# A new written order for a fused gated-attention and MLP kernel: the same steps at other places in the engines' queues

## The chip, the cores and the metric

The kernel runs on one core of one Trainium2 chip. Its engines take their instructions from separate queues, each strictly in order, and wait for one another by semaphores: PE multiplies matrices, DVE and POOL work elementwise, ACT applies functions and copies, SP issues transfers. The metric is the device time of one execution in microseconds (us). Times are given as the median of several executions. Beside them stands one execution under the profiler, and all durations of single instructions come from it.

## The reference

Two stages, in float32. A gated linear attention carries a 48 x 48 state for each of 4 x 8 (batch, head) pairs through 768 tokens; its output, put back as 3072 tokens of 384 numbers, goes through an MLP whose activation is `h * cos(h)`.

```python
B, H, S, D = 4, 8, 768, 48
for t in range(S):
    state = alpha[:, :, t, :, None] * state + einsum('bhd,bhe->bhde', k[:, :, t], v[:, :, t])
    y[:, :, t] = einsum('bhd,bhde->bhe', q[:, :, t], state)
x = y.transpose(0, 2, 1, 3).reshape(3072, 384)
h = x @ w_in            # 384 x 2048
out = (h * cos(h)) @ w_out      # 2048 x 384
```

## The kernel before

The 3072 tokens are cut into 12 jobs J0 to J11 of 256 tokens (three for each batch). A job holds two chunks of 128 rows; in J0 and J1, which are loaded together in another layout, a digit in a step's name after the kind can also mean a quarter or a half of the heads. Every piece of work is a named step, a small function that issues one or some instructions:

- `load a/k/q/v` (SP, lines 124 and 134) brings in the inputs of a job, 384 KB each; `w1` and `w2` (POOL's transfer queue, lines 150 and 156) bring in four parts of each weight, u0 to u3.
- `ln` (ACT, line 174) takes the logarithm of alpha; `mula` (POOL, line 180) first multiplies neighbouring gates. `cq`, `cd`, `cums0`, `cums` (PE) sum the logarithms with triangular matrices, `sub` (DVE, line 239) forms a difference. `icp` and `exps` (ACT, lines 250 and 256) take exponentials; `eb` stands for a job's four exponentials and the next job's `ln`.
- `sk` and `sq` (lines 269 and 273) multiply k and q by these exponentials: 128 x 384 float32, both operands in SBUF. `:D` after a date puts a step on DVE, `:A` on ACT; without a letter `sk` and `sq` run on POOL. `castv` (line 283) converts v.
- `trans` (PE, lines 342 and 352) transposes the scaled q and k, `evT` (lines 359 and 362) evicts the result, `scores` (PE, line 370) multiplies them, `mask` (DVE, line 375) masks the scores. `vpe` and `vev` (lines 301 to 316), or `vst` by transfers (SP, line 289), stack v.
- `outer` (PE), `decay` (POOL, line 325), `add` (DVE, line 411) and `state` (line 420) carry the state from chunk to chunk. `yT` (PE, line 446) makes the attention's output, `evy` (line 456) evicts it.
- `m1 u` (PE, line 465, 12 matmuls of 256 columns), `sin u` (ACT, line 471, on 128 x 1024), `gate u` (DVE, line 476) are the first half of the MLP; `m2` (PE, lines 487 and 493, 4 matmuls of 384 columns each) is the second, `evo` (lines 500 and 502) evicts it and `out` (SP, line 510) stores it. `idle` (PE, line 518) multiplies zeros.

What decides the order is the table `PLAN`: for each step one date per job, `-` where a job has no such step. The program sorts all steps by date and issues them so; a date is only a key for sorting, and nothing waits for a date. Each engine then runs its instructions in that order, and the tile framework adds the semaphores.

```python
    with tc.manual_schedule():
        for _, _, kind, args in sorted(order, key=lambda x: x[:2]):
            steps[kind](*args)
```

Two pools of PSUM matter for waiting. Tag `h` has three slots of two banks, shared by T_ps, A_ps, U_ps, y_ps and the MLP's h_ps, so that an `m1` can only begin when the step that reads an older slot is done. Tag `o` has one slot: the next `m2` chain begins when `evo` has emptied it. A wait is kept per tile: a writer of one half of a two-bank tile waits for earlier readers of the other half.

Of the kernel before, what the change touches and what calls it, by code (L numbers as in the profile page):

```python
# [16 lines left out]
def kernel(  # L17
# [11 lines left out]
    B, H, S, D = q.shape  # L29
# [78 lines left out]
    w1 = consts.tile([C, KT, DF], BF, tag="w1", name="w1")  # L108
    w2 = consts.tile([C, NF, DM], BF, tag="w2", name="w2")
# [404 lines left out]
    def idle(n):  # L514
# [18 lines left out]


    PLAN = {
# [73 lines left out]
    }  # L609
    IDLE = [(1201, 11), (5915, 1), (9015, 20), (13611, 2), (18367, 3)]  # L610

    order = []
    for key, line in PLAN.items():
        kind, *rest = key.split()
        for J, word in enumerate(line.split()):
            if word != "-":
                t, _, eng = word.partition(":")
                args = [J] + [int(x) if x.isdigit() else x for x in rest] + [{"A": "ACT", "D": "DVE", "P": "POOL"}[x] for x in eng]
                order.append((int(t), len(order), kind, args))
    for t, n in IDLE:  # L620
        order.append((t, len(order), "idle", [n]))
# [34 lines left out]
```

## Time and profile before

| what | value |
|---|---|
| median of 3 executions | 193.19 us (190.25, 193.44, 193.19) |
| the profiled execution, its own time | 190.47 us |
| its span, first to last instruction | 188.8 us |
| granted PE clock, mean | 0.996 |
| PE busy | 178.0 us, 94% of the span |
| DVE busy | 136.1 us, 72% |
| ACT busy | 128.8 us, 68% |
| POOL busy | 75.3 us, 40% |
| moved by transfers | 29.48 MB, mean 156 GB/s |

The span is what the profile divides into instructions; the execution's own time is 1.7 us longer. Busy shares are averages over the whole span. An engine with 72% can be full in one stretch and idle in another, so the profile is read by stretches of time, and after that by what an engine waited for.

### The profile page before, as it was taken

Reading aid. Unit: us, or ns where it says so; the run is one execution under the profiler, and the core shown is the slowest. Engines: PE = TensorE matmul, PEld = TensorE weight load, DVE = VectorE, ACT = ScalarE, POOL = GpSimd, SP = SyncE. Lnnn points to the kernel's source line nnn. Section 1 sums busy time; section 2 is a strip of 40 time slices with the busy share of each in tenths; the row PEclk is TensorE's granted clock in tenths of the full one; section 3 lists DMA queues with packets and bytes.
Section 4 is the critical chain, followed back from the end, with each engine's and each line's share of the span. In section 5 each row is a group of like instructions: output and inputs, shape, how many; then the busy total and the mean of one; then the engine's idle time right before and its main releaser. Section 6 shows DMA issues by size and latency. Waiting matters only on the chain.

```text
span 188.8 us, 5950 instructions
## 1 busy us (share of the span) xinstructions
PE 178.0 (94%) x2543; PEld 129.7 (69%) x2546; DVE 136.1 (72%) x183; ACT 128.8 (68%) x166; POOL 75.3 (40%) x111
## 2 busy tenths in 40 slices
PE   7898989989999999999999999999999999999990
PEld 2555776846578686786688668576686686777770
DVE  7086887657998989488978987978558686562640
ACT  4374685799689989889778999547844573373530
POOL 7085900167749163584494089070620501000000
PEclk9999999999999999999999999999999999999998
DMA  5979999999978849959998874034050000450313
GB/s 173 320 207 144 198 174 153 265 283 244 318 193 230 230 122 244 256 139 288 233 286 235 225 181 121 9 69 115 23 120 2 5 0 3 107 119 11 77 41 83
DMA packets 56570, 29.48 MB, mean 156 GB/s; under 512 B 43360, under 2 KB 56544, under 8 KB 56544
## 3 DMA queue, kind: packets, MB, share of 16 engines
q1 hardware_dynamic: 52672, 25.86, 51.8%
q0 software_dynamic: 3712, 3.15, 11.2%
q8 instruction: 20, 0.33, 0.7%
q10 hardware_dynamic: 160, 0.10, 0.2%
q14 instruction: 6, 0.05, 0.1%
HBM read 25.17 MB, written 4.72 MB: 158 GB/s over the span
## 4 chain that ended last, share of the span: by engine, by line
PE 72%; ACT 10%; DVE 8%; DMA 4%; issue 2%; SPq 1%; DVEq 0%; ACTq 0%
PE h_ps L465 31%; PE o_ps L493 26%; PE y_ps L446 5%; DMA q<-in_q_dram 4%; PE A_ps L370 2%; DVE kh L269 2%; ACT c_sb L471 2%; DVE gsb L476 2%; PE T_ps L352 2%; PE U_ps L398 2%; DVE xT L456 2%; PE o_last L487 1%; ACT cp L256 1%; ACT L165 1%; ACT L471 1%
## 5 line engine op out<-in xcount | busy, mean ns | idle before, releaser
L476 DVE TENSOR_TENSOR gsb<-h_ps,c_sb 128x1024 bf16<-128x1024 f32 x48 | 58.3, 1222 | 20.2 <-ACT c_sb L471 18.6
L471 ACT ACTIVATE c_sb<-h_ps,halfpi 128x1024 bf16<-128x1024 f32 x48 | 53.1, 1113 | 21.8 <-PE h_ps L465 21.2
L493 PE MATMUL o_ps<-w,gsb 128*128 128x384 bf16 x368 | 66.7, 326 | 0.9 <-DVE o_sb L502 0.6
L465 PE MATMUL h_ps<-xT,w 128*128 128x256 bf16 x576 | 66.2, 272 | 1.2 <-ACT xT L456 0.7
L465 PEld LDWEIGHTS <-w 128*128 128x128 bf16 x576 | 55.7, 98 | 9.8 <-issue 1.7
L493 PEld LDWEIGHTS <-gsb 128*128 128x128 bf16 x368 | 33.9, 98 | 22.0 <-issue 1.3
L375 DVE TENSOR_TENSOR A_sb<-A_ps,msk 128x1024 bf16<-128x1024 f32 x24 | 28.8, 1214 | 1.9 <-PE A_ps L370 1.9
L420 POOL TENSOR_TENSOR un<-us,c 128x384 bf16<-128x384 f32 x16 | 14.0, 873 | 35.5 <-DVE us L411 35.5
L273 POOL TENSOR_TENSOR qh<-q,cp 128x384 bf16<-128x384 f32 x15 | 14.9, 999 | 13.1 <-DMA q<-in_q_dram 13.1
L273 POOL TENSOR_TENSOR kh<-k,icp 128x384 bf16<-128x384 f32 x15 | 15.2, 1021 | 4.3 <-ACT icp L250 4.3
L180 POOL TENSOR_TENSOR a<-a 128x384 f32<-128x384 f32 x9 | 9.3, 1031 | 15.3 <-DMA a<-in_alpha_dram 15.3
L502 ACT COPY o_sb<-o_ps 128x384 f32<-128x384 f32 x12 | 5.8, 480 | 12.6 <-PE o_ps L493 9.6
L362 ACT COPY qkT<-T_ps 128x1024 bf16<-128x1024 bf16 x10 | 9.7, 1017 | 3.6 <-DVE qkT L362 2.1
L518 PE MATMUL idle_ps<-zeros 128*128 128x512 bf16 x34 | 10.5, 461 | 1.7 <-DVE zeros L53 1.3
L456 DVE CAST xT<-y_ps 128x384 bf16<-128x384 f32 x13 | 7.0, 553 | 6.4 <-ACT xT L456 4.5
L174 ACT ACTIVATE lna<-a 128x768 bf16<-128x768 f32 x12 | 10.1, 846 | 2.1 <-DMA a<-in_alpha_dram 2.1
L165 ACT ACT_TABLE_LOAD x8 | 10.3, 1283 | 0.9 <-PEq L640 0.8
L471 ACT ACT_TABLE_LOAD x8 | 10.3, 1283 | 0.1
L411 DVE TENSOR_TENSOR us<-U_ps,un 128x384 f32<-128x384 f32 x16 | 8.8, 552 | 1.8 <-PE U_ps L398 1.8
L502 DVE COPY o_sb<-o_ps 128x384 f32<-128x384 f32 x11 | 6.1, 553 | 5.5 <-PE o_ps L493 5.5
L370 PE MATMUL A_ps<-qkT 48*128 48x128 bf16 x192 | 9.0, 218 | 1.1 <-DVE gsb L476 0.4
L370 PEld LDWEIGHTS <-qkT 48*128 48x128 bf16 x192 | 5.8, 94 | 4.8 <-issue 2.6
(91 smaller groups left out, 179.1 us busy)
## 6 DMA issues: line engine op xcount, KB each, us to landing
a<-in_alpha_dram SPq DMA_DIRECT2D x12, 384.0 KB, 4.7
q<-in_q_dram SPq DMA_DIRECT2D x12, 384.0 KB, 5.2
k<-in_k_dram SPq DMA_DIRECT2D x12, 384.0 KB, 5.5
v<-in_v_dram SPq DMA_DIRECT2D x12, 384.0 KB, 4.5
out_dram<-o_sb SPq DMA_DIRECT2D x38, 96.0 KB, 2.2
vs<-vp SPq DMA_DIRECT2D x36, 64.0 KB, 2.6
w<-in_moe_w_in_dram POOLq DMA_DIRECT2D x4, 384.0 KB, 6.3
w<-in_moe_w_out_dram POOLq DMA_DIRECT2D x4, 384.0 KB, 8.0
```

The lines of the kernel that those rows point to most:

```text
L165: nc.scalar.preload_act_table_set("natural_log_exp_and_others")
L273: eng.tensor_tensor(out=x[J % NQ][:, e, :, 0:D], in0=kqv[nm, J][:, :, e], in1=f, op=ALU.mult)
L370: nc.tensor.matmul(A_ps[J, c][:, a, p, :], qkT[r, c, NP + p, :], qkT[r, c, p, :], start=True, stop=True)
L375: nc.vector.tensor_tensor(out=A_sb[J][:, c].rearrange("s a p t -> s (a p) t"), in0=A_ps.pop((J, c)).rearrange("s a p t -> s (a p) t"), in1 ...
L420: eng.tensor_tensor(out=u, in0=new, in1=c2_sb[J][:, :, c].unsqueeze(3).to_broadcast([C, NP, 2, D]), op=ALU.mult)
L456: copy(out=xT[J][:, :, c * C : (c + 1) * C], in_=y_ps[J][:, c, 0 : KT * C].rearrange("r (i t) -> r i t", i=KT))
L465: nc.tensor.matmul(h_ps[J, u][:, f, :], w1[:, kk, ft * C : (ft + 1) * C], xT[J][:, kk, :], start=(kk == 0), stop=(kk == KT - 1))
L471: nc.scalar.activation(out=c_sb[J, u], in_=h_ps[J, u], func=AF.Sin, bias=halfpi, scale=1.0)
L476: nc.vector.tensor_tensor(out=gsb[J][:, u * FW : (u + 1) * FW], in0=h_ps.pop((J, u)), in1=c_sb.pop((J, u)), op=ALU.mult)
L493: nc.tensor.matmul(o_ps[J, c][:, 0:DM], gsb[J][:, ft, c * C : (c + 1) * C], w2[:, ft], start=(ft == 0), stop=(ft == NF - 1))
L502: copy(out=o_sb[J, c], in_=o_ps.pop((J, c))[:, 0:DM])
L518: nc.tensor.matmul(idle_ps[0], zeros[:, 0:C], zeros, start=True, stop=True)
```

## The change

Only the dates in `PLAN`, the letters behind them and the list `IDLE` are others; every function stays, and every step of before is there once. PE has one more matmul of zeros (38 for 37). On PE the order differs up to about date 48,000, the beginning of `yT J2`; behind it PE's steps stand in the same order to the end. On the other engines steps change their places throughout, and forty change the engine: ten of `sk` and `sq` go from POOL to DVE and four from DVE to POOL, `castv J2` goes from POOL to ACT, thirteen evictions go from DVE to ACT and twelve from ACT to DVE. SP issues loads in another order relative to the stores, and POOL issues the parts of the weights as u2, u3, u0, u1 and u0, u3, u2, u1 (before: u2, u0, u1, u3 and u0, u1, u2, u3). The core of the diff:

```diff
     PLAN = {
...
-        "load a": "750 1320 27620 28190 29330 37741 44441 56807 66187 68447 74447 82487",
-        "w1": "10835 12726 9645 13576",
-        "w2": "17133 18763 19613 20463",
-        "sub": "- - - 39720 45836 51846 61530 76810 84617 92106 106190 119199",
-        "icp 0": "6915 9600 37604 - - - - - - - - -",
-        "exps 0": "7290 8725 38854 - - - - - - - - -",
-        "sk 0": "9210:D 11254:D 38651:D 41651 48351 66435:D 71598 82909 94573 107068 109918 129216",
-        "sk 1": "10718:D 11968:D 39049 42535:D 53753 63201 77427 81983:D 90096 108018 108968 131692:D",
-        "sq 0": "8545 8545:D 40192 43621:D 49851 65101 72548 87426 89566:D 110996:D 118996 128266",
-        "sq 1": "11685 9926:D 40195:D 43151:D 52803 62251 76307 88376 91123 103448 117876 130336",
-        "castv": "11710:A 13291:A 35881 46851 55551 57441 78377 92853 89326 106298 119946 141140",
-        "vev": "- - 41200 - - - - - - - - -",
-        "vev 1": "16476:A 21611 - - - - - - - - - -",
-        "decay": "10665 10495 40022 42601 56321 77257 79147 82739 104398 118826 130166 127316",
-        "evT 0": "13831 18156:A 42569:A 45891:A 59319 70018:A 83329:A 91501 110391 115839 129342 140188:A",
-        "yT": "19166 26750 48173 56676 71150 89916 89286 107371 123000 135506 148672 161541",
-        "evy 0": "20016 27740 49163:D 57764:D 72140 90906 90486 108361:D 123990 138375:D 149785 162531:D",
-        "evy 1": "19996:D 27740:D 49163 58844:D 72140:D 90906:D 90116 108836:D 123990:D 137900:D 150155 162531",
-        "m1 2": "24684 32304 52639 59692 77257 95330 102636 118310 131457 147259 156839 163732",
-        "m2 0 0": "26002 39990 55275 69096 82407 99284 113085 124915 136231 149557 160793 172269",
-        "m2 0 1": "27635 40643 55928 69749 83060 99937 113738 125568 136884 150210 162426 173580",
-        "evo 0": "35128:D 44102 62005:D 76847 85519:D 103388:D 117117 127727:D 139043 153109:D 165903 176392",
-        "evo 1": "39400 53847 68076:D 81387:D 89091:D 109916:D 123105 131657 142875 158049 170773:D 177718:D",
-    IDLE = [(1201, 11), (5915, 1), (9015, 20), (13611, 2), (18367, 3)]
...
+        "load a": "750 1320 26317 26887 27457 38218 44218 52518 61318 64288 82764 84534",
+        "w1": "14036 15056 9465 11916",
+        "w2": "17823 22193 21343 19713",
+        "sub": "- - - 39020 46278 51887 62196 77467 85827 92763 106847 126262",
+        "icp 0": "8690 8315 37557 - - - - - - - - -",
+        "exps 0": "6915 9440 39878 - - - - - - - - -",
+        "sk 0": "9635:D 11362:D 38489:D 42578:D 54278 62180 73272:D 84902:D 95544 106605 111877 127387",
+        "sk 1": "10493:D 12653:D 39495:D 42128:D 53328 59340 79082:D 82640:D 91144 107555 109197 129087:D",
+        "sq 0": "8195 8195:D 41231:D 43628:D 55228 65859:D 72255 88053 89003 110147 118533 128337",
+        "sq 1": "12766 10780 40781:D 44078:D 49628 64269:D 74155 89376:D 92094 104105 119856:D 129287",
+        "castv": "11710:A 13862:A 39128:A 47288 48128 61240 76868 94774 90374 105835 119483 130727",
+        "vev": "- - 42515:A - - - - - - - - -",
+        "vev 1": "17228:A 21133:A - - - - - - - - - -",
+        "decay": "14886 18673 46248 46078 62010 78588 78758 83396 108505 120253 130557 131497",
+        "evT 0": "15028 18903:A 43265:A 46548:A 59976 71298 83986:A 92158 110573 116496 127877 140845:A",
+        "yT": "19856 25447 48830 57333 71807 90573 89943 108028 123657 136163 149329 162198",
+        "evy 0": "20763 26523:D 49820 58421:D 72797:D 91563:D 90773 109018:D 124647 137646 150442 163188",
+        "evy 1": "20686:D 26560 49822:D 59501:D 72797 91563 90773:D 109493:D 124647:D 137276 151723:D 163558",
+        "m1 2": "26985 32257 53296 60349 77914 95987 103293 118967 132114 147916 157496 164389",
+        "m2 0 0": "26332 41021 55932 69753 83064 99941 113742 125572 136888 150214 161450 172926",
+        "m2 0 1": "33575 41674 56585 70406 83717 100594 114395 126225 137541 150867 163083 174237",
+        "evo 0": "35734:D 44503 61721:D 77504 86176 104045:D 117774 128384 139700 153766 166560 177049:D",
+        "evo 1": "40306:D 49347:D 68733:D 82044:D 89748 111178:D 125017 132337:D 143532 158636:D 171430:D 178375:D",
+    IDLE = [(1201, 11), (5913, 1), (9013, 23), (15816, 1), (19117, 2)]
...
```

96 rows, old and new, of the table PLAN are left out of this document.

## The prediction

> **What bounds the kernel now.** I read busy time by engine, then windows by stretch, then PE's waits, then the timeline of the places where the order changes. First the page, with three windows for PE alone (start:end, length, busy, instructions, granted clock, DMA share, GB/s):
>
> ```profile
> PE 178.0 (94%) x2543; PEld 129.7 (69%) x2546; DVE 136.1 (72%) x183; ACT 128.8 (68%) x166; POOL 75.3 (40%) x111
> ...
> 24.27:55.00 30.73, 28.95 (x423) 1.00 1.03 238
> 55.00:80.00 25.00, 24.86 (x368) 1.00 0.82 214
> 80.00:184.50 104.50, 103.43 (x1437) 1.00 0.43 109
> ```
>
> At 24.27 us PE begins `m1 0 J0`. From there to 184.5 us it is busy for 28.95 + 24.86 + 103.43 = 157.2 of 160.2 us. A new order neither adds nor removes a matmul there, so the most it can gain behind 24.27 us is PE's idle time, 3.0 us or 1.6%. What it can lose has no such bound. PE's waits from 24 us on, in all (waiter, releaser, total us, times, longest):
>
> ```profile
> PE h_ps L465 <- ACT xT L456: 0.7, 2, 0.5
> PE o_ps L493 <- DVE o_sb L502: 0.6, 1, 0.6
> PE A_ps L370 <- DVE gsb L476: 0.4, 1, 0.4
> PE h_ps L465 <- DVE xT L456: 0.4, 1, 0.4
> ```
>
> All are single short waits for an eviction or a gate. The next question is which engine stands close behind PE. Windows with PE, PEld, DVE, ACT and POOL busy:
>
> ```profile
> 40.00:50.00 10.00, 9.44 (x141) 5.96 (x140) 8.31 (x12) 8.05 (x16) 7.14 (x9) 1.00 1.03 277
> 50.00:60.00 10.00, 9.82 (x162) 7.66 (x160) 9.07 (x11) 8.90 (x13) 5.71 (x7) 1.00 0.92 237
> 60.00:70.00 10.00, 10.00 (x154) 7.39 (x153) 9.15 (x12) 9.56 (x12) 4.62 (x7) 1.00 0.62 165
> ```
>
> DVE has 1.69 + 0.93 + 0.85 = 3.5 us left in 30. Its share of 72% over the span hides this. Last, what a scaling step costs on DVE, alone and beside POOL (start, us):
>
> ```profile
> 42.71 0.56 DVE L273 TENSOR_TENSOR kh<-k,icp 128x384 bf16<-128x384 f32 x1 [0.75 <-ACT icp L250]
> 47.39 1.31 POOL L180 TENSOR_TENSOR a<-a 128x384 f32<-128x384 f32 x1
> 47.76 1.35 DVE L273 TENSOR_TENSOR qh<-q,cp 128x384 bf16<-128x384 f32 x1
> ```
>
> The same shape takes 0.56 us alone and 1.35 us when it begins during POOL's `mula`. It ends 0.4 us behind it, as if it had waited for POOL. On POOL the step takes 1.0 us.
>
> **The change part by part.**
>
> *Start.* In the new order `cd` writes a tile that `icp 0 J1` reads, and stands behind it. Following the rows (one `cq` 0.33 us to issue and 0.5 to end, an exponential 0.49): `cq 1 1 J0` waits for `exps 0 J0` until 8.36, `cq 1 1 J1` ends at 9.85, `icp 0 J1` runs to 10.37, and `cd` ends at 10.96 instead of 10.63. Behind it stand 23 `idle` matmuls for 20:
>
> ```profile
> 10.71 4.26 PE L518 MATMUL idle_ps<-zeros 128*128 128x512 bf16 x19
> 14.90 0.46 PE L342 MATMUL T_ps<-ident_bf,kh 64*128 64x64 bf16 x10
> 15.66 0.34 PE L342 MATMUL T_ps<-ident_bf,kh 64*128 64x64 bf16 x6 [0.29 <-DVE kh L269]
> ```
>
> From 10.63 to 14.90 they take 0.214 us each, so `trans J0` begins at 10.96 + 23 x 0.214 = 15.9 and, with 1.08 us for its 32 matmuls (as `trans J1`), ends at 16.95 instead of 16.5: +0.5. By then DVE has one scaling less to do (`sq 1 J1` is on POOL), but POOL does `sq 1 J1`, `w1 u3`, `sq 1 J0` from 12.5 on: 1.0 to 1.3, 0.8, 1.0 to 1.3, ending at 15.3 to 15.9, or 16.6 if it also waits for DVE. So +0.5, up to +0.8. The two `idle` behind `trans J0` go and one comes before `scores`; there PE waits for `evT` anyway. Before `yT J0` one `idle` fewer: -0.2. `m1 0 J0` begins at +0.3, with 0 and +0.9 as the ends.
>
> *`yT J1` and `evo`.* Before, `yT J1` is followed by 0.65 us of `m2` and then a wait of 0.43 us for `evy`. Now `m2 0 0` and `m1 2 J0` (0.65 + 1.35) cover both evictions. But `yT J1` now needs the `h` slot of `gate 0 J0`, and `m1 0 J1` that of `gate 3 J0`. Walked through with 1.11 for `sin`, 1.22 for `gate`: `yT J1` at 28.75, `m1 1 J1` at 31.7, `m2 1 0 J0` at 39.7 against 39.75. The +0.3 is repaid: -0.3, ends -0.4 and 0. The eviction wait of 0.65 us before `m2 1 0 J0` stays.
>
> *J2 and J3 on DVE.* From 42.1 us on DVE gains `sk 1 J2`, `sq 0 J2`, `sk 0 J3`, `evo 1 J0` and `evo 1 J1`, five times 0.56, and loses `vev J2` (0.94): +1.9 us. `vev J2` is now on ACT, where the shape is not shown; the nearest rows are `castv` (128 x 768, 0.83) and `evT` (128 x 1024, 1.02), and I take 0.9. With 0.56 for each, DVE ends `sq 1 J3` at 48.3; before it was 49.12. With the 0.8 us of two meetings with POOL (`mula J5`, `state 0 J2`) it is 49.9. Queued behind are `evT 1 J2`, `mask 0 J2`, `sub J4`, `mask 1 J2`; `yT J2` waits for the last, then `m1 1 J2`. So -0.5 to +1.6; I take +0.6, as the meetings are likely but POOL has less to do. The cover is ACT's `evT 0 J2` at 48.4, for which `scores 0 J2` waits in any case.
>
> *J5 between the gates.* `sq 1 J5` and `sq 0 J5` stand between the gates of J3, while `sk 0 J5` (0.55) leaves. Two times 0.56 makes `gate 1 J3` end at 73.8 where `trans J5`, 73.6 before, waits for it; `evo 1 J2`, `add 0 J4` and `mask 0 J4` are behind. I take +0.3; with nothing met it is 0, with both at 1.35 it is +1.6.
>
> *Loads and weights.* The gate on `load a J2` is `yT J1`, 1.6 us earlier; with the stores behind the loads, `load a J7` comes at some 51 us (61.1 before). PE's list shows no wait for a load, so 0. `w1 u0` and `u1` are now issued third and fourth. The third and fourth landed at 21.5 and 23.4 us, needed at 24.5 and 25.9: 0. `w2 u1`, last, landed at 33.3 and is needed at 37.1: 0.
>
> *Behind 80 us.* `sq 0 J9` and `sub J11` (0.55 each) leave DVE ahead of the 0.45 us wait at 121.9 us for a gate; `evo 0/1 J4` go to ACT, which was idle for 2.4 us there. I take -0.2, ends -0.9 and +0.5 (a new wait of that size). The last `evo` are hidden under `m2`.
>
> Sum: +0.3 - 0.3 + 0.6 + 0.3 - 0.2 = +0.7 us. Against the profiled execution that is 190.47 + 0.7 = 191.2. This execution lies low: the three runs are 190.25, 193.19 and 193.44. I cannot say which level the next median takes, so I put the sum on the mean of the four known executions, 191.8: 192.5.
>
> [...]
>
> **The rivals.**
>
> 1. *DVE becomes the bound from 42 to 76 us (slower).* Its additions there, seven times 0.56 and `evT 0 J5` at 0.69, less `vev J2` and `sk 0 J5`, are 3.1 us. If all five scalings meet POOL, they cost 5 x 0.8 = 4.0 more. 7.1 less the 3.5 us that DVE has free is +3.6, all on PE by `mask`, `gate` and `evo`: 191.8 + 3.6 = 195.4, from the median 196.8. It decides once DVE is full in these windows. For it: 8.3 to 9.2 of 10 now. Against: POOL loses five of these steps and gains one, so there are fewer meetings. 17%.
> 2. *The new order of the weights makes PE wait.* If `w1 u0` and `u1` land 2 us behind the third and fourth of before, `m1` begins 1 to 2 us late: 193.5. For it: two scalings stand between POOL's issues. Against: over 1.5 us of slack. 8%.
> 3. *The order recovers what PE waits for.* With loads 10 us earlier and fewer evictions on DVE, all 3.0 us of idle time might go: 191.8 + 0.3 - 3.0 = 189.1. Against: new waits for slots. 7%.
> 4. *The start alone counts*: PE's order behind `yT J2` is the same, nothing else shows, and the start is not repaid: +0.9, or 192.7. 13%.
>
> **How the numbers follow.** The forecast has 55%. Its own ends add to -1.8 and +4.6 us, which all come together rarely. The range takes 190.25 less 0.75 and 193.44 plus 2.3: 189.5 to 195.7. Outside are most of rival 1 at its median price and half of rival 3. About 2% (3.9 us) is what a measurement of this kernel can tell from no change. Slower by more: rival 1 fully developed (10%), a late weight (1%), the rest (2%), 13%. Faster by more: half of rival 3 and a low level of the runs, 5%. Within: 82%.
>
> **What would show it.** Right: `trans J0` ends 0.4 to 0.8 us later, `m1 1 J1` begins at 31.5 to 32.5 with no wait before it, `yT J2` begins between 52.7 and 53.9, DVE's share in 40 to 60 us is above 9, and PE's last matmul ends within 1.5 us of before. Wrong: a PE wait over 1 us between 40 and 76 us, a wait for `w1`, or PE's idle time behind 24 us under 1.5 us.

## The result, and the profile after

The new order takes 191.96 us (median of 18 executions, 190.32 to 194.31), the old one 191.70 us on the same chip (18, 189.37 to 193.45). The ratio is 1.0056, 95% interval 1.0029 to 1.0084: slower by 0.56%, some 1.07 us of 190. In some executions of either kernel the mean granted PE clock is 0.982 or less (in the traces of after it then falls to half for about 7 us near 20 us) and the time is some 3 us longer; the ratios here leave these out, so they are not quotients of the medians.

The page of after shows such a fall (busy time of two engines, and the granted clock in 40 slices of 4.8 us):

```profile
PE 181.6 (94%) x2547; PEld 131.8 (69%) x2547; DVE 139.0 (72%) x188; ACT 129.1 (67%) x168; POOL 68.5 (36%) x104
...
PEclk9999579999999999999999999999999999999998
```

I read the steps from a second profiled execution of the same kernel (called "after again" below), whose clock fell for a shorter time (from 20 to 27 us its mean is 0.76, that of the page above 0.52): own time 191.84 us, span 190.0, mean granted clock 0.987. PE alone in the three windows of before:

```profile
24.27:55.00 30.73, 29.23 (x427) 1.00 1.04 247
55.00:80.00 25.00, 24.72 (x371) 1.00 0.85 221
80.00:184.50 104.50, 103.03 (x1432) 1.00 0.42 104
```

That is 156.97 us of 160.2, against 157.2 before, so PE is idle for 3.3 us of it. Counted from 24.68 us, where `m1 0 J0` begins here, to 185.2 it is 157.47 of 160.52 us, or 3.05 idle. The 3.0 us of idle time of before, the most that the order could have recovered, is still there. The longest of PE's waits in this stretch:

```profile
PE o_ps L493 <- DVE o_sb L502: 0.6, 1, 0.6
PE h_ps L465 <- DVE gsb L476: 0.5, 1, 0.5
PE A_ps L370 <- DVE gsb L476: 0.5, 1, 0.5
PE T_ps L352 <- DVE qh L273: 0.4, 1, 0.4
```

The second line is new: an `m1` that waits for a gate. Before, `m1` waited only for evictions (`xT`). No wait is for a weight or a load. The windows from 40 to 70 us (PE, PEld, DVE, ACT, POOL):

```profile
40.00:50.00 10.00, 9.36 (x147) 5.86 (x145) 9.68 (x15) 8.44 (x16) 4.39 (x6) 1.00 1.05 285
50.00:60.00 10.00, 9.83 (x155) 7.49 (x154) 9.07 (x12) 8.32 (x12) 5.28 (x6) 1.00 0.88 230
60.00:70.00 10.00, 10.00 (x155) 7.39 (x153) 9.14 (x13) 9.49 (x12) 4.65 (x6) 1.00 0.71 183
```

DVE went from 8.31 to 9.68 in the first window, POOL from 7.14 to 4.39, and PE lost only 0.08 there.

To find where the time went, I compared the beginning of each PE step with before. The columns are "after again" less before, in us, so a change from row to row is gained or lost between them:

| PE step | before | after again | difference |
|---|---|---|---|
| first `cq` | 5.93 | 4.98 | -0.94 |
| `scores 1 J0` | 18.30 | 17.95 | -0.35 |
| `m1 0 J0` | 24.27 | 24.68 | +0.41 |
| `m1 1 J1` | 32.40 | 31.62 | -0.78 (order of steps differs) |
| `m2 1 0 J0` | 39.75 | 39.69 | -0.06 |
| `yT J2` | 52.87 | 53.12 | +0.25 |
| `m2 0 0 J4` | 87.77 | 88.02 | +0.25 |
| `outer J5` | 90.86 | 90.99 | +0.13 |
| `m1 0 J5` | 99.40 | 99.54 | +0.14 |
| `m1 2 J5` | 100.71 | 101.48 | +0.76 |
| `m2 1 3 J11`, the last step | 183.66 | 184.43 | +0.78 |

The first `cq` begins anywhere from 4.98 to 5.93 us in the profiled executions of this study, the same kernel included. The start must therefore be counted from it. Counted so, every later row stands 0.94 us higher, the last at +1.72. Some 1.1 us of this is the fallen clock: `m1 0 J0` then stands at +1.36, and at +0.27 in a trace of this order whose clock held (mean 0.994, "after with the fill" below, which has nine more matmuls of zeros). So the column shows where time is lost from row to row; that its last entry of +0.78 is near the measured 1.07 is chance.

Behind `yT J2` the difference moves at two places only: -0.12 at `outer J5` and +0.62 at `m1 2 J5`. The latter is as large as the loss of the start (0.60 at `scores 1 J0`), and the prediction does not have it. Its place in "after again" (timeline of PE and ACT; in brackets the wait before the instruction and what ended it):

```profile
97.26 0.48 ACT L456 CAST xT<-y_ps 128x384 bf16<-128x384 f32 x1 [1.09 <-DVE xT L456]
97.76 1.28 ACT L471 ACT_TABLE_LOAD   x1
99.05 3.12 ACT L471 ACTIVATE c_sb<-h_ps,halfpi 128x1024 bf16<-128x1024 f32 x3
...
101.48 2.78 PE L465 MATMUL h_ps<-xT,w 128*128 128x256 bf16 x24 [0.46 <-DVE gsb L476]
```

and in before:

```profile
95.55 1.26 ACT L456 CAST xT<-y_ps 128x384 bf16<-128x384 f32 x3 [2.41 <-PE y_ps L446]
96.83 1.28 ACT L471 ACT_TABLE_LOAD   x1
98.29 1.11 ACT L471 ACTIVATE c_sb<-h_ps,halfpi 128x1024 bf16<-128x1024 f32 x1 [0.18 <-PE h_ps L465]
```

Before, ACT evicted `evy 1 J6`, `evy 0 J6` and `evy 0 J5` one behind another, and DVE had only the last, `evy 1 J5`. In the new order DVE has `evy 1 J6` and `evy 0 J5`, and ACT's `evy 1 J5`, which writes the other half of the same `xT`, waits 1.09 us for DVE. Behind it on ACT stand the table load of 1.28 us and every `sin` of J6. Taken against `m1 0 J5`, the first `sin` comes 0.62 us later (99.05 - 99.54 against 98.29 - 99.40); so does its `gate`, and `m1 2 J5` needs the slot that the gate frees.

### The profile page after: what moved, and what is told of

Same layout as the page of the kernel before. It is cut to its first block, busy times and chain, and to the rows that moved or that the text cites. A ratio compares the mean times of both kernels' runs of the same rounds, so it can differ in the third digit from the quotient of the medians.

```text
span 192.4 us, 5952 instructions
## 1 busy us (share of the span) xinstructions
PE 181.6 (94%) x2547; PEld 131.8 (69%) x2547; DVE 139.0 (72%) x188; ACT 129.1 (67%) x168; POOL 68.5 (36%) x104
## 4 chain that ended last, share of the span: by engine, by line
PE 77%; ACT 11%; DVE 8%; issue 2%; DVEq 0%; ACTq 0%
PE h_ps L465 29%; PE o_ps L493 26%; PE idle_ps L518 6%; PE y_ps L446 5%; ACT c_sb L471 2%; DVE gsb L476 2%; PE A_ps L370 2%; ACT L471 2%; DVE xT L456 2%; PE cums_h L198 2%; ACT xT L456 2%; PE T_ps L342 1%; PE o_last L487 1%; DVE qh L273 1%; ACT L165 1%
## 5 line engine op out<-in xcount | busy, mean ns | idle before, releaser
L420 POOL TENSOR_TENSOR un<-us,c 128x384 bf16<-128x384 f32 x16 | 13.5, 846 | 41.6 <-DVE us L411 41.6
L273 POOL TENSOR_TENSOR qh<-q,cp 128x384 bf16<-128x384 f32 x12 | 12.6, 1053 | 8.9 <-ACT cp L256 8.9
L273 POOL TENSOR_TENSOR kh<-k,icp 128x384 bf16<-128x384 f32 x11 | 10.9, 1001 | 10.5 <-ACT icp L250 10.5
L518 PE MATMUL idle_ps<-zeros 128*128 128x512 bf16 x38 | 11.8, 465 | 1.3 <-DVE zeros L53 1.3
L362 ACT COPY qkT<-T_ps 128x1024 bf16<-128x1024 bf16 x9 | 8.9, 1022 | 3.7 <-DVE qkT L362 2.1
L502 ACT COPY o_sb<-o_ps 128x384 f32<-128x384 f32 x11 | 5.3, 479 | 8.6 <-PE o_ps L493 8.5
L456 ACT CAST xT<-y_ps 128x384 bf16<-128x384 f32 x12 | 5.5, 478 | 7.6 <-DVE xT L456 4.5
L456 DVE CAST xT<-y_ps 128x384 bf16<-128x384 f32 x12 | 6.5, 552 | 5.3 <-PE y_ps L446 3.4
```

The source lines that it names most:

```text
L273: eng.tensor_tensor(out=x[J % NQ][:, e, :, 0:D], in0=kqv[nm, J][:, :, e], in1=f, op=ALU.mult)
L420: eng.tensor_tensor(out=u, in0=new, in1=c2_sb[J][:, :, c].unsqueeze(3).to_broadcast([C, NP, 2, D]), op=ALU.mult)
L456: copy(out=xT[J][:, :, c * C : (c + 1) * C], in_=y_ps[J][:, c, 0 : KT * C].rearrange("r (i t) -> r i t", i=KT))
L518: nc.tensor.matmul(idle_ps[0], zeros[:, 0:C], zeros, start=True, stop=True)
```

## Experiments

The theory after these traces: the order itself costs the time, with a start 0.6 us longer and the eviction order of J5 (0.6 us) as the two losses, 0.5 us repaid at `yT J1`, and little between. Its rivals: the scalings on DVE in J2 to J5 are what costs (as the prediction had it), or the fall of the clock is. In the expectations A is the theory of the order, and other letters are its rivals.

### After again, twice

The kernel of after, unchanged, for another profile.

> The new order once more, for a profile in which the granted clock does not dip near 20 us. Theory A (the loss is made in the start and at the evictions of J5): against the profile of before PE's steps stand +0.6 us at scores 1 J0, about +0.1 at m2 1 0 J0 after the repayment at yT J1, +0.1 from yT J2 to m2 0 3 J4, and jump by +0.6 at m1 2 J5 to +0.6 to +0.8, where they stay. Rival B (the scalings on DVE, as the prediction had it): the offset grows by 0.6 between 42 and 55 us and by 0.3 between 68 and 76 us, and does not jump at m1 2 J5.

One execution, 194.26 us, with the same fall of the clock (mean 0.977). Its steps agree with the first profile's up to `m2 1 0 J0` (+2.48 us in both), `yT J2` is 0.2 us later.

> The new order as it is, for a profile at full granted clock. Counted from the first cq matmul, to take out when the warm-up matmuls end, theory A expects against before: scores 1 J0 +0.6 us, m1 0 J0 +0.4, m2 1 0 J0 -0.1, yT J2 +0.2, m1 1 J6 +0.1, m1 2 J5 +0.7, and +0.7 at the last matmul; a ratio near 1.005. Rival B expects most of the growth between 42 and 76 us.

Median 191.84 us (9 executions), ratio 1.0044 [1.0008, 1.0079], the profile used above. The two ratios of after agree. Counted from the first `cq`, `scores 1 J0` stands at +0.60 as expected, and the step of 0.62 at `m1 2 J5` is there; the levels in between and at the end (+1.36 at `m1 0 J0`, +1.72 at the last step) are not those of theory A, because the clock fell again (0.76 from 20 to 27 us). From 42 to 76 us the difference grew by 0.31, not by the most of it as rival B has it.

### Twenty matmuls of zeros instead of 23

```diff
-    IDLE = [(1201, 11), (5913, 1), (9013, 23), (15816, 1), (19117, 2)]
+    IDLE = [(1201, 11), (5913, 1), (9013, 20), (15816, 1), (19117, 2)]
```

> The new order with 20 matmuls of zeros behind cd in place of 23. Theory A: the idle matmuls set the begin of trans J0 (15.97 us in the profile after, while its last input from DVE is there at 15.65 and from POOL at 15.23), so trans J0 ends at about 16.5 in place of 17.07, all behind it moves by 0.5 us, and the time falls by 0.5 us, to a ratio of 1.003 to the kernel before. Rival (the start is repaid at yT J1 whatever its length): no change, 1.0056. Rival C (fewer busy matmuls make the clock dip more often): the fast runs as theory A, but the share of slow runs rises.

The profiled execution took 190.29 us (span 188.6). Counted from the first `cq`, `scores 1 J0` begins at 12.38 us: before 12.37, after 12.97. So three matmuls of zeros (3 x 0.214 = 0.64) account for the 0.59 us that the start lost; the inputs of `trans J0` were ready for the earlier date. The matmuls of zeros ahead of it, in "after again" and in this run:

```profile
9.96 5.12 PE L518 MATMUL idle_ps<-zeros 128*128 128x512 bf16 x23
...
10.09 4.48 PE L518 MATMUL idle_ps<-zeros 128*128 128x512 bf16 x20
```

From `m1 0 J0` to `m2 1 0 J0` this trace gains 0.48 us on before, "after again" 0.47, so the later repayment does not shrink with the start. A ratio could not be had: in five of six executions the clock fell (mean 0.978 or 0.979). That fewer matmuls of zeros let it fall more often is therefore not refuted.

### The evictions of J5 exchanged

```diff
# evy 0, J5
-91563:D
+91563
# evy 1, J5
-91563
+91564:D
```

> The new order, but of yT J5's two evictions the first is on ACT and the second on DVE, as before. Theory A: ACT no longer waits 1.1 us for DVE ahead of the table load, sin 1 J6 begins 0.6 us earlier, m1 2 J5 no longer waits for gate 1 J6 (0.46 us), and the time falls by 0.6 us, to a ratio of 1.002 to 1.003. Rival B: the wait only moves on, no change: 1.0056.

Ratio 0.999 [0.9971, 1.0009]. The step of 0.62 us is gone: `m1 0 J5` and `m1 2 J5` stand at the same +3.59 us against before (an execution with a fallen clock, mean 0.973, so the level is not comparable, the step is). The wait on ACT, in the timeline:

```profile
99.92 0.48 ACT L456 CAST xT<-y_ps 128x384 bf16<-128x384 f32 x1 [0.30 <-PE y_ps L446]
...
101.88 1.11 ACT L471 ACTIVATE c_sb<-h_ps,halfpi 128x1024 bf16<-128x1024 f32 x1 [0.18 <-PE h_ps L465]
```

ACT waits 0.30 us for PE instead of 1.09 for DVE, and `sin` follows PE again as before. Two dates take this step back. The ratio lies below the 1.002 to 1.003 of theory A. Against after's 1.0044 and 1.0056 it gains 1.0 to 1.25 us, and the trace shows 0.62 of it. The intervals leave room for the step alone; whether there is more stays open, as only four of the twelve executions enter the ratio.

### The same evictions, put into the order of before

```diff
# evy 0 and evy 1, J5
-90906      90906:D
+90906:D    90907
# evy 0 and evy 1, J6
-90486      90116
+90116      90116:D
```

> The kernel before with one part of the change alone: the evictions of yT J6 and yT J5 go to the engines as in the new order (first of J5 on DVE, second on ACT). Theory A: ACT waits for DVE ahead of the table load, sin 1 J6 begins 0.6 us later, PE waits 0.46 us or more ahead of m1 2 J5: +0.6 us, a ratio of 1.003. Rival (the wait is harmless in the order of before): 1.000.

Ratio 1.0042 [0.9999, 1.0085]; the interval touches 1. In the trace `m1 2 J5` loses 0.62 us (-0.84 to -0.22 against before), and PE and ACT show the same two waits:

```profile
96.28 0.48 ACT L456 CAST xT<-y_ps 128x384 bf16<-128x384 f32 x1 [1.09 <-DVE xT L456]
...
100.49 3.76 PE L465 MATMUL h_ps<-xT,w 128*128 128x256 bf16 x33 [0.46 <-DVE gsb L476]
```

This one part of the change, alone, makes the step. With the run above it is shown both ways.

### Both edits

Twenty matmuls of zeros and the evictions exchanged.

> Both edits: 20 idle matmuls and the evictions of J5 as before. Theory A: the two add, -1.1 us, a ratio of 0.999 to 1.000 to the kernel before. Rival B: 1.0056, as the scalings on DVE stay where they are.

The profiled execution took 189.86 us. Counted from the first `cq`, its last matmul is 0.48 us earlier than in before (1.17 as the raw date), with no step at `m1 2 J5`. The ratio of 1.0163 [1.0141, 1.0186] says nothing on the order: in six of seven executions the mean granted clock was 0.973 to 0.982.

### Five scalings back on POOL

`sk 1 J2`, `sq 0 J2`, `sk 0 J3`, `sq 1 J5` and `sq 0 J5` of after without the letter D.

> The new order with the five scalings of J2 to J5 (sk 1 J2, sq 0 J2, sk 0 J3, sq 1 J5, sq 0 J5) back on POOL at the same dates. Rival B (these scalings on DVE are what costs): -0.5 to -1.0 us, a ratio of 0.996 to 1.001. Theory A (DVE has room for them where they stand): no gain; 1.0056 or slower, since a scaling takes POOL 1.0 us in place of 0.56 and POOL already does two casts there.

Ratio 1.0035 [1.0001, 1.0068]: not to be told from after's 1.0044 and 1.0056. In the trace `yT J2` comes 0.30 us earlier against `m2 1 0 J0` than in before, where "after again" has it 0.31 later. In J5 nothing moves, and the 0.62 us at `m1 2 J5` stays. So the scalings of J5 cost nothing, and those of J2 and J3 up to 0.6 us in the trace.

### Both edits and PE's waits filled

The kernel with both edits, and matmuls of zeros where PE waited in the start:

```diff
-    IDLE = [(1201, 11), (5913, 1), (9013, 20), (15816, 1), (19117, 2)]
+    IDLE = [(1201, 11), (5913, 1), (7064, 2), (8400, 3), (9013, 20), (15816, 3), (19117, 2), (21300, 2)]
```

> Both edits of e3 (20 idle matmuls behind cd, the evictions of J5 as before), and matmuls of zeros in four places where PE waits: 2 ahead of cq 1 1 J0, 3 ahead of cd, 2 more ahead of scores 1 J0, 2 ahead of m1 0 J0. Theory C (the granted clock falls for some 7 us near 20 us because PE does too little just before; the fall costs 3 us): the fall becomes rarer, and the time is 189.4 to 190 us, a ratio of 0.997 to 1.000. Rival (the fall has to do with the kind of matmuls, or with nothing in PE's gaps): as e3, with medians at 193 us. If the added matmuls were on the path, the time would rise by up to 9 x 0.21 = 1.9 us.

Median 189.74 us (188.7 to 190.43, 12 executions) against 190.32 for before: ratio 0.9967 [0.9944, 0.999]. It beats both kernels, and in none of its executions did the clock fall (mean 0.994 to 0.999). Three edits at once do not say which of them gains; the next three runs bear on that.

### The fill in before, and in after

Before with the same nine matmuls of zeros in its own waits (two of them ahead of `scores 1 J0`, two ahead of `m1 0 J0`):

> The order of before, with 9 more matmuls of zeros (46 for 37) in the places where PE waits in the start: 2 and 3 ahead of the later cq, 2 ahead of scores 1 J0, 2 ahead of m1 0 J0. The question is what the fill does by itself, since the kernel that beat before (ratio 0.9967) had the fill, 20 idle matmuls and the two evictions of J5 exchanged at once. Theory A (the gain of that kernel over before is the order of after, 0.5 us at yT J1 and 0.1 at evo J4, with the start and the evictions mended): the fill alone gives nothing, ratio 0.999 to 1.003, trace offset 0 to +0.3 us, since it only stands where PE waited. Theory C (the fill keeps PE busy and so keeps the granted clock, which falls to half for some 7 us near 20 us in some executions): the profiled execution shows no fall in the PEclk row, the times of the single runs lie within 1.5 us of one another, and the median comes out 0.3 to 1.5 us below that of before.

Ratio 1.0039 [1.0017, 1.0062], median 190.73 against 190.26. Both theories missed. The clock did hold in all ten executions (mean 0.994 to 1.0), which lie within 1.24 us, but the fill costs 0.7 us: more than the 0.24 us by which `m1 0 J0` comes later, counted from the first `cq` (18.58 against 18.34). Where the rest goes stays open.

After with the fill alone, 23 matmuls of zeros and evictions as they are (47 such matmuls in all; the 44 in the text below is the count of the kernel with 20):

> After with its 23 idle matmuls ahead of trans J0 and its evictions of J5 as they are, and only the fill of PE's waits in the start (44 matmuls of zeros for 38). Theory A (the 3 idle matmuls cost up to 0.6 us and the eviction order of J5 costs 0.6 us, both untouched here): slower than the kernel that has the fill and these two mended by 0.6 to 1.2 us, that is a ratio to before of 1.000 to 1.003, and the jump of 0.6 us at m1 2 J5 is in the trace. Theory C (the mean cost of after is mostly the fall of the clock): ratio 0.996 to 0.998, the same as the kernel with both mended, whatever the trace shows at m1 2 J5.

Ratio 1.0034 [1.0008, 1.006]. So filling gives after no gain beyond its interval (1.0044, 1.0056), and theory C, which gave 0.996 to 0.998, falls: 1.0034 is just above what theory A gave, and with the clock held (mean 0.993 to 1.0), after still is slower than before as it is, by 0.65 us. Against before with the same fill it is not slower: the medians of the two, from the same chip, are 190.80 and 190.73 us. The fill costs before 0.7 us and after nothing that shows, and why is open; so the slowdown is shown for the two kernels as they are, and not for the two orders with the fill in both.

The kernel with the same fill and the two edits is at 0.9967. The difference, 0.0067 or 1.27 us, agrees with the 0.65 of three matmuls of zeros plus the 0.62 of the evictions, but each ratio is known to some 0.5 us only. These two losses are as large as the slowdown of after, or larger; what the order repays elsewhere is the rest. The profiled execution, with 190.20 us one of the shorter of the ten, does not show the sum: counted from the first `cq`, its last step is 0.40 us earlier than in before, and that of the kernel with the two edits 0.57.

What hides it is that this trace has the J2 and J3 stretch in another way. "After again" first (timeline of DVE, POOL and PE):

```profile
45.12 1.82 DVE L273 TENSOR_TENSOR kh<-k,icp 128x384 bf16<-128x384 f32 x2
...
47.34 1.65 DVE L273 TENSOR_TENSOR qh<-q,cp 128x384 bf16<-128x384 f32 x2
...
45.25 1.28 POOL L180 TENSOR_TENSOR a<-a 128x384 f32<-128x384 f32 x1 [7.39 <-DMA a<-in_alpha_dram]
...
49.05 0.38 PE L352 MATMUL T_ps<-ident_bf,qh 64*128 64x64 bf16 x14 [0.42 <-DVE qh L273]
```

and after with the fill:

```profile
44.58 1.02 DVE L273 TENSOR_TENSOR kh<-k,icp 128x384 bf16<-128x384 f32 x2
...
45.19 1.28 POOL L180 TENSOR_TENSOR a<-a 128x384 f32<-128x384 f32 x1 [7.47 <-DMA a<-in_alpha_dram]
...
47.89 0.40 PE L352 MATMUL T_ps<-ident_bf,qh 64*128 64x64 bf16 x16
```

DVE issues the same two scalings. Where POOL's `mula J5` begins just behind the first, the pair takes 1.82 us and `trans J3` waits 0.42; where it begins behind the start of both (the second starts near 45.0), the pair takes 1.02 and PE does not wait. `yT J2` is then 0.68 us earlier than in before, counted from `m2 1 0 J0`, instead of 0.09 to 0.32 later in the seven other traces of this order. Two more traces of this order fit: in the kernel with both edits and the fill `mula J5` begins 0.07 us behind the start of the pair, which takes 1.83 us ("after again": 0.13 behind, 1.82; here: 0.61 behind, 1.02). In the first profile of after it begins 1.81 us ahead of the pair, which takes 1.05, and meets the two `sq` of J2 instead: that pair takes 1.57 us, here 1.02. `mula J5` waits for a transfer in all four (as in the brackets, POOL idle for 7.17 to 7.47 us), so in these traces the landing of that transfer sets which scaling it meets. Why a scaling takes longer there is not shown.

### The faster kernel with three scalings on POOL

The kernel with both edits and the fill, `sk 1 J2`, `sq 0 J2` and `sk 0 J3` without the letter D.

> The kernel with 20 idle matmuls, fill and the evictions of J5 exchanged, and besides sk 1 J2, sq 0 J2 and sk 0 J3 back from DVE to POOL as in before. In the run with the scalings on POOL, yT J2 came 0.3 us earlier against m1 1 J1 than with them on DVE, but its ratio could not be told from that of after. Theory A (these three scalings cost 0.3 us on DVE): yT J2 begins 0.2 to 0.5 us earlier, counted from m1 1 J1, than in the kernel without this edit, and the ratio to before is 0.994 to 0.996. Rival: the wait goes to another step ahead of yT J2, and the ratio stays at 0.9967 within its interval.

Ratio 0.9986 [0.9965, 1.0008]: no gain over 0.9967, the intervals overlap, and theory A's 0.994 to 0.996 is missed. `yT J2` comes 0.60 us earlier against `m1 1 J1` than in the kernel without this edit, as expected in kind; but after with the fill has these scalings on DVE and does better still (from `m1 1 J1` to `yT J2`, against before: +0.04 us there, +0.43 here, +1.03 without this edit). The place of the three scalings is not worth a gain that these times can show.

## Why the prediction was right or wrong

**The number, and the level it was put on: wrong.** The sum of +0.7 us had the sign and the size: 0.56% is 1.07 us, interval 0.55 to 1.6. But the sum was put on 191.8, a mean of the four executions known, and gave 192.5, which is below the median of 193.19 that the next measurement was to be set against. Read as a forecast it said 0.7 us faster, against its own working. The failed step is "I put the sum on the mean of the four known executions".

**The start: right.** Predicted +0.5 at the end of `trans J0` (16.95 us). In the profile of after, whose first `cq` is at 5.93 us as before, it is 17.08; counted from the first `cq` every step up to `scores 1 J0` is 0.60 later. For `m1 0 J0` +0.3 was predicted; with the clock held (after with the fill, nine more matmuls of zeros) it is +0.27. The price was the matmuls of zeros, as said, and POOL's late `sq` did not add to it.

**`yT J1` and `evo`: right, a little small.** Predicted were 28.75, 31.7 and 39.7 us for `yT J1`, `m1 1 J1` and `m2 1 0 J0`; "after again" has 28.75, 31.62 and 39.69, with no wait before `m1 1 J1`. That these dates agree to 0.1 us is luck: the execution began its first `cq` 0.94 us earlier than before and lost about as much to its clock. Counted from the first `cq`, with the clock held (after with the fill), the three steps are 0.2 to 0.3 us earlier than predicted. From `m1 0 J0` to `m2 1 0 J0` the repayment is 0.47 us, predicted 0.3. In this timeline of PE the wait for `evy` is gone and that for `evo` stays:

```profile
28.75 0.52 PE L446 MATMUL y_ps<-qkT,un 128*32 128x128 bf16 x24
...
30.31 6.78 PE L465 MATMUL h_ps<-xT,w 128*128 128x256 bf16 x60
...
39.69 0.81 PE L493 MATMUL o_ps<-w,gsb 128*128 128x384 bf16 x4 [0.65 <-DVE o_sb L502]
```

**J2 and J3 on DVE: right mechanism, size too large.** Predicted +0.6 (-0.5 to +1.6); measured +0.31 and, in seven traces of eight, 0.09 to 0.32, in one -0.68. DVE's 9.68 and 9.07 are above 9. Both meetings that were named took place in "after again": `sk 0 J3` took 1.36 us beside `mula J5`, and `sq 1 J3` 1.19 beside `state 0 J2` (0.55 alone; the rows of 1.82 and 1.65 us). With both, DVE ended `sq 1 J3` at 48.99 us, where the prediction had 49.9. Less 0.80 and 0.63 for the meetings that is 47.6, against the 48.3 worked out for DVE alone: there the term was too large. `yT J2` at 53.12 us lies in the interval given, but as a raw date by the same luck as above; from the terms measured it is 52.87 + 0.27 - 0.47 + 0.31 = 52.98, which lies in it too.

**J5 between the gates: size wrong.** Predicted +0.3, measured 0.00: the difference is +0.25 us at every step from `yT J2` to `m2 0 0 J4`. Two scalings of 0.56 us found room, and moving them to POOL changed nothing.

**Loads and weights: right.** No wait for either, although the weights' parts come in another order.

**Behind 80 us: wrong.** Predicted -0.2, measured -0.12 at `outer J5` and +0.62 at the evictions of J5, together +0.5, the far end of the bounds given. Neither reason given for the -0.2 shows: the wait for a gate, 0.45 us at 121.9 us before, is 0.46 at 122.64 in "after again", and `outer J5` begins within 0.1 us of `evo 0 J4` in both traces, so it does not come behind it; what the 0.12 is stays open. The failed step is that this part counted DVE's load and the `evo`, and did not walk through what stands on ACT between `yT J5` and the first `sin`: an eviction that waits for DVE, and a table load behind it. That PE's order was the same there was taken as cover; ACT's was not.

So the sum came out by luck, by two errors that cancel: J2, J3 and J5 0.6 to 0.8 too high, the stretch behind 80 us 0.7 too low. The traces add up to +0.6 us (0.27 - 0.47 + 0.31 - 0.12 + 0.62), less than the 1.07 of the ratio. Three of the ten executions behind that ratio have a mean clock of 0.986 or 0.987, as "after again" has, and took 191.57 to 192.19 us; the other seven average 190.72, which is 0.74 above the 189.98 of the nine of before. So some 0.3 of the 1.07 us goes with a short fall of the clock, for which the prediction had no term.

**A scaling beside a `w1` issue: no term in the sum.** In the trace of before the `kh` on DVE at 12.98 us takes 1.35 us, with a `w1` issue from 13.07 to 13.87. In the same trace the `kh` at 11.54 us takes 0.54 us, all of it beside another such issue (11.14 to 12.08). So an issue by itself need not hold up a scaling; what held the one at 12.98 is not shown.

**The rivals.** DVE did not become the bound: its windows are above 9, yet PE's longest wait behind `m2 1 0 J0` and up to 76 us is 0.4. No weight came late, and the 3.0 us of idle time stayed. The rival "the start alone counts" gives nearly the measured time (+0.9), but not for its reason: the start was repaid, and the evictions of J5 took as much again.

## What to carry to other kernels

When steps change engines, walk through what stands behind each of them on the new engine, table loads included (1.28 us here), up to the step that PE waits for; two evictions that changed engines cost 0.62 us that no busy share shows. Two instructions that write halves of one tile from two engines are a chain if the framework keeps waits per tile (1.09 us of waiting here): the half that is computed last should not stand ahead of work that the next stage needs. A sum worked out against one execution is a difference: add it to the level that the next measurement will be compared with, and let no other choice of level turn its sign.

## What the hardware showed unexpectedly

The granted clock can fall in the middle of a busy kernel. PE in a window of after (busy us, count, granted clock, DMA share, GB/s), and of after with the fill:

```profile
20.00:27.00 7.00, 6.93 (x138) 0.52 1.14 168
```

```profile
20.00:27.00 7.00, 6.53 (x141) 1.00 1.21 178
```

At 0.52 a group of 32 matmuls of `yT J0` takes 1.07 us for 0.62, and `m1 0 J0` begins 21.29 us behind the first `cq` instead of 18.61. PE's longest wait before that was 0.7 us. With nine more matmuls of zeros in the short waits around it, the mean granted clock was at 0.99 or above in all 42 executions of the four kernels so filled; of after's 28 executions, 13 had 0.980 or less. The fill costs time itself: 0.7 us in before, against the executions whose clock held.

What makes the clock fall is not shown. From 5 to 12 us PE is busy for 5.75 of 7 us in after and for 6.75 with the fill, but in the run with twenty matmuls of zeros it is also busy for 5.75, and there the clock from 20 to 27 us is 1.00.
